# A GpSimd copy ahead of w_in's loads: issuing weights behind the turned k of batch 0

## Chip, cores and metric

One core of a Trainium2 chip. The metric is the device time of one execution in microseconds (us). The span of a profile is some 2 us shorter than the time of the same execution.

## The reference

Pooled attention, then a GELU layer. Inputs are float32.

```python
# q, k, v: (8 batches, 8 heads, 576, 64);  w_in: (512, 2048);  w_out: (2048, 512)
k_p, v_p = mean of k, v over groups of 8 rows              # 72 rows each
attn = softmax(q @ k_p.T / 8)
x = (attn @ v_p), heads side by side                       # (4608, 512)
out = gelu_tanh(x @ w_in) @ w_out
```

## The kernel before

Batch 0's attention runs alone at the start. Then 9 groups of 512 rows go through the two products, with the attention of the next batch in between. Weights are cast to bf16 by the DMAs that GpSimd issues; k and v of batch 0 come over the queues of SyncE and ScalarE.

```python
load_k(0, [nc.sync, nc.scalar])
load_v(0, [nc.sync, nc.scalar])
load_q(0, 0, 1)                       # GpSimd, as all loads down to w_out
load_q(0, 1, 2)
make_identity(nc, identb)
load_w_in(0)                          # first half of w_in: rows 0 to 255, used first
load_w_in(1)                          # second half
load_k(1, [nc.gpsimd])
load_q(1)
for i in range(4):                    # w_out in four parts
    nc.gpsimd.dma_start(out=w_out_b[...], in_=w_out_v[:, i])
# ...
trans_k_mm(0, 4, 0, KR, D)
trans_k_copy(0, 0, 4, upper=False)    # VectorE writes kTs[0][0]: the first part of the turned (transposed) k
trans_q(0, ...)
trans_k_copy(0, 1, 4, upper=False)
scores(0, 0, 2)
# ... scores, exponentials, denominators ...
for f in v_steps(0): f()              # VectorE adds up v
av0(0, 0, 4)                          # PE: attention times v (L368)
# ...
for i in range(2):
    nc.vector.memset(vts[1][:, 2 * i, 0:1], 0.0)
load_v(1, [nc.sync], 2)               # v of batch 1, issued once these memsets are done
for fo, ko in [(fo, ko) for fo in range(6) for ko in range(2)]:
    p1_mm(0, fo, ko)                  # 12 products with w_in's first half (L402)
# group 0 goes on with ko 2 and 3: w_in's second half; then p2_mm with w_out (L411)
```

The softmax here doesn't subtract the row's maximum and nothing guards it: scores larger than these inputs give would overflow.

Of the kernel before, what the change touches and what calls it, by code (L numbers as in the profile page):

```python
# [18 lines left out]
def kernel(  # L19
# [9 lines left out]
    nc = tc.nc  # L29
# [39 lines left out]
    def load_k(b, engs):  # L69
        rows = k[b].rearrange("h (j l) d -> (h j) (l d)", l=8)  # L70
        main = rows[0:128 * KR].rearrange("(p r) c -> p r c", r=KR)
        n = KR // len(engs)
        for i, eng in enumerate(engs):
            eng.dma_start(out=kts[b % 2][:, i * n:(i + 1) * n], in_=main[:, i * n:(i + 1) * n])
        engs[0].dma_start(out=kts[b % 2][64:128, KR], in_=rows[128 * KR:])
        rows = v[b].rearrange("h (j l) d -> j h (l d)", l=8)
        engs[-1].dma_start(out=kts[b % 2][0:64, KR], in_=rows[64:])  # L77
# [18 lines left out]
    def load_q(b, i0=0, i1=2):  # L96
        if b not in qs:
            qs[b] = qp.tile([128, 2, T * D], BF16, name="qb")
        nc.gpsimd.dma_start(
            out=qs[b][:, i0:i1],  # L100
            in_=q[b].rearrange("(i h) (p t) d -> (h p) i (t d)", i=2, t=T)[:, i0:i1])
# [3 lines left out]
    w_out_b = consts.tile([128, FO, DM], BF16, name="w_out_b")  # L105
    w_in_v = moe_w_in.rearrange("(ko p) f -> p ko f", p=128)
    w_out_v = moe_w_out.rearrange("(q p j) d -> p q (j d)", p=128, j=4)
# [9 lines left out]
    def load_w_in(i):  # L117
        nc.gpsimd.dma_start(out=w_in_b[i], in_=w_in_v[:, 2 * i:2 * i + 2])

    load_w_in(0)  # L120
    load_w_in(1)
    load_k(1, [nc.gpsimd])
    load_q(1)
    for i in range(4):
        nc.gpsimd.dma_start(out=w_out_b[:, 4 * i:4 * i + 4, :].rearrange("p j d -> p (j d)"), in_=w_out_v[:, i])
    gate = consts.tile([1, 2], BF16, name="gate")


    xT = consts.tile([128, KO, N], BF16, name="xT")

    kTs = [[consts.tile([128, H, Sp], BF16, name=f"kT{i}{e}") for e in range(2)] for i in range(2)]
# [78 lines left out]
    def half_bank(bank):  # L210
        return PS[:, bank, :].bitcast(BF16)
# [7 lines left out]
    def trans_k_copy(b, e, bank, lower=True, upper=True):  # L219
        tp = half_bank(bank)[0:D, 0:(KR + 1) * 128].rearrange("p (r c) -> p r c", c=128)  # L220
        o = kTs[b % 2][e][e * 64:(e + 1) * 64]

        def heads(h0, h1, n, c0, c1):
            nc.vector.tensor_copy(out=o[:, h0:h1, 0:n].rearrange("p h (j r) -> p h j r", r=KR),
                                  in_=tp[:, 0:KR, c0:c1].rearrange("p r (h j) -> p h j r", h=h1 - h0))

        if lower:
            heads(0, 4, Sp, 0, 4 * KH)
        if upper:
            heads(4, H - 1, Sp, 4 * KH, 7 * KH)  # L230
            heads(H - 1, H, 8, 7 * KH, 128)
            nc.vector.tensor_copy(out=o[:, H - 1, 8:Sp], in_=tp[:, KR, 64:128])
# [22 lines left out]
    def trans_q(b, i, t0, n, bank, eng):  # L255
        trans_q_mm(b, i, t0, n, bank)
        trans_q_copy(b, i, t0, n, bank, eng)
# [11 lines left out]
    def qk(b, c, pr, bank):  # L269
        for e in range(2):  # L270
            h = 2 * pr + e
            nc.tensor.matmul(out=PS[:Sp, bank + e, :CH].rearrange("j (t p) -> j t p", p=32),  # L272
                             lhsT=kTs[b % 2][c][:, h],
                             rhs=qTs[b][:, h // 4, :, h % 4 * 32:h % 4 * 32 + 32],
                             start=True, stop=True)

    def expo(b, c, pr, bank):
        e = ep.tile([Sp, 2, CH], BF16, name="e", bufs=8)
        nc.scalar.activation(out=e, in_=PS[:Sp, bank:bank + 2, :CH], func=ACT.Exp, scale=1.0 / 64.0)  # L279
        es[b, c, pr] = e  # L280
# [157 lines left out]
    def scores(c, pr, bank):  # L438
        qk(0, c, pr, bank)
        expo(0, c, pr, bank)  # L440
# [3 lines left out]
    trans_q(0, *QG[0], 5, nc.scalar)  # L444
    trans_q(0, *QG[1], 6, nc.vector)
    trans_k_copy(0, 1, 4, upper=False)
    scores(0, 0, 2)
    scores(0, 1, 0)
    spin(2, 7)
# [55 lines left out]
    for g in range(NG):  # L505
# [41 lines left out]
        if g + 1 == NG:  # L547
# [3 lines left out]
            for i, o in enumerate(gLs):  # L551
                side[4 * i + 3].append(lambda i=i, o=o: nc.vector.tensor_copy(  # L552
                    out=o.rearrange("p f (x t) -> p f t x", t=4),
                    in_=gTs[g][:, 4 * i:4 * i + 4, 384:].rearrange("p f (t x) -> p f t x", t=4)))
# [130 lines left out]
```

## Time and profile before

| | before |
|---|---|
| median of 3 runs | 301.98 us (301.66 to 302.01) |
| PE busy | 291.7 of 300.3 us |
| v of batch 0 landed | 16.3 us |
| first product with w_in | 21.25 us |
| w_in's halves landed | 17.1 and 23.1 us |

A DMA is finished when 16 engines have counted its semaphore up. The trace keeps the time of each count, so "landed" is the 16th, and where the 15th is given as well, the difference is how far one engine lags. "PE waits" are idle times of the engine just ahead of an instruction. The prediction shows the lines.

### The profile page before, as it was taken

How to read it: one execution, taken by the hardware profiler on the slowest of the kernel's cores; microseconds unless marked ns; L12 is line 12 of the kernel's file. 1: busy time of each engine (PE TensorE's matmuls, PEld its weight loads, DVE VectorE, ACT ScalarE, POOL GpSimd, SP SyncE). 2: the span in 40 equal slices, each digit the busy share in tenths (PEclk: the TensorE clock that was granted, in tenths of full speed). 3: DMA queues.
4: the chain of work that ended last, by engine and by line, in shares of the span. 5: the costliest groups of instructions: out<-in, count | busy, mean ns of one | idle time of the engine just before them, and what ended most of it. 6: DMA issues, size and time to landing. Idle time of an engine off the chain costs nothing.

```text
span 300.3 us, 4352 instructions
## 1 busy us (share of the span) xinstructions
PE 291.7 (97%) x1496; PEld 151.0 (50%) x1525; DVE 152.7 (51%) x308; ACT 217.1 (72%) x408; POOL 37.5 (12%) x67
## 2 busy tenths in 40 slices
PE   8889999999999999999999999999999999999995
PEld 3555545554555455545554555455545555445443
DVE  3766585574576257815690659155924630111112
ACT  1687678879888898789878988798879887206500
POOL 7104002300600060005000410033000000000000
PEclk9999999999999999999999999999999999999999
DMA  7999985981799269935984499729961210121022
GB/s 225 265 249 272 248 172 105 248 210 16 181 259 179 38 159 252 183 68 123 258 191 87 92 255 208 106 51 250 238 120 38 69 42 0 36 71 36 0 62 80
DMA packets 38790, 43.11 MB, mean 144 GB/s; under 512 B 25520, under 2 KB 26160, under 8 KB 38640
## 3 DMA queue, kind: packets, MB, share of 16 engines
q0 software_dynamic: 8000, 24.39, 35.7%
q1 hardware_dynamic: 30064, 17.06, 25.2%
q10 hardware_dynamic: 704, 1.38, 1.4%
q8 instruction: 12, 0.20, 0.3%
q14 instruction: 10, 0.08, 0.1%
HBM read 36.70 MB, written 9.44 MB: 154 GB/s over the span
## 4 chain that ended last, share of the span: by engine, by line
PE 91%; DMA 5%; DVE 2%; issue 1%; ACTq 1%
PE PS L402 41%; PE PS L411 39%; DMA vt<-in_v_dram 5%; PE PS L327 4%; PE PS L316 2%; PE PS L647 1%; DVE vt L154 1%; PE PS L301 1%; PE PS L368 1%; PE PS L292 1%; PE PS L272 0%; ACTq L77 0%; PE PS L241 0%; DVE xT L345 0%; PE PS L354 0%
## 5 line engine op out<-in xcount | busy, mean ns | idle before, releaser
L411 PE MATMUL PS<-w_out_b,gT 128*128 128x512 bf16 x543 | 134.7, 379 | 0.9 <-issue 0.2
L402 PE MATMUL PS<-xT,w_in_b 128*128 128x512 bf16 x565 | 125.7, 379 | 0.6
L408 ACT ACTIVATE gT<-PS 128x512 bf16<-128x512 f32 x144 | 79.6, 606 | 44.6 <-PE PS L402 44.6
L402 PEld LDWEIGHTS <-w_in_b 128*128 128x128 bf16 x576 | 65.0, 113 | 58.5
L411 PEld LDWEIGHTS <-gT 128*128 128x128 bf16 x560 | 53.9, 97 | 51.1 <-issue 1.7
L345 DVE TENSOR_TENSOR xT<-PS,rc 64x288 bf16<-64x288 f32 x112 | 51.0, 455 | 21.2 <-ACT rc L337 18.7
L417 DVE COPY osb<-PS 128x512 f32<-128x512 f32 x33 | 22.8, 692 | 48.1 <-PE PS L411 44.8
L322 ACT ACTIVATE eT<-PS 64x576 bf16<-64x576 f32 x48 | 30.7, 640 | 0.6
L309 DVE COPY eT<-er 8x576 bf16<-8x576 bf16 x24 | 7.3, 302 | 39.4 <-ACT er L307 38.9
L334 ACT ACTIVATE ld<-PS 64x288 f32<-64x288 f32 x56 | 22.5, 403 | 5.6 <-PE PS L327 5.1
L337 ACT ACTIVATE rc<-ld 128x288 f32<-128x288 f32 x56 | 24.8, 443 | 1.8
L379 ACT ACT_TABLE_LOAD x17 | 21.8, 1283 | 3.6 <-issue 3.3
L154 DVE TENSOR_TENSOR kt<-kt 128x1280 f32<-128x1280 f32 (+5 forms) x18 | 18.9, 1048 | 10.0 <-DMA kt<-in_v_dram 5.9
L335 ACT ACTIVATE ld<-PS 64x288 f32<-64x288 f32 x56 | 22.5, 403 | 1.4
L327 PE MATMUL PS<-eT,vp 72*128 72x288 bf16 x96 | 19.7, 285 | 0.1
L154 DVE TENSOR_TENSOR vt<-vt 128x512 f32<-128x512 f32 (+2 forms) x18 | 15.6, 865 | 2.1 <-DMA vt<-in_v_dram 1.8
L512 POOL COPY gate<-eT 1x2 bf16<-1x2 bf16 x5 | 0.9, 176 | 125.4 <-DMA eT<-er 125.4
L327 PEld LDWEIGHTS <-vp 72*128 72x128 bf16 x96 | 9.5, 98 | 11.3
L279 ACT ACTIVATE e<-PS 72x576 bf16<-72x576 f32 x16 | 9.9, 645 | 3.1 <-PE PS L272 2.9
L431 PE MATMUL PS<-idle 128*128 128x512 bf16 x30 | 9.9, 476 | 1.3 <-DVE idle L143 1.2
L316 PE MATMUL PS<-qT,kx 128*128 128x288 bf16 x48 | 9.8, 286 | 0.0
L552 DVE COPY kt<-gT 128x512 bf16<-128x512 bf16 x4 | 3.0, 747 | 11.5 <-ACT gT L408 11.5
(66 smaller groups left out, 131.0 us busy)
## 6 DMA issues: line engine op xcount, KB each, us to landing
out_dram<-osb SPq DMA_DIRECT2D x141, 64.0 KB
kt<-in_k_dram POOLq DMA_DIRECT2D x12, 512.0 KB, 6.2
vt<-in_v_dram POOLq DMA_DIRECT2D x12, 512.0 KB, 10.5
qb<-in_q_dram POOLq DMA_DIRECT2D x7, 576.0 KB, 14.4
w_in_b<-in_moe_w_in_dram POOLq DMA_DIRECT2D x2, 1024.0 KB, 16.7
w_out_b<-in_moe_w_out_dram POOLq DMA_DIRECT2D x4, 512.0 KB, 24.3
kt<-in_k_dram POOLq DMA_DIRECT2D x1, 1024.0 KB, 22.1
vt<-in_v_dram SPq DMA_DIRECT2D x4, 256.0 KB
```

The source lines that it names most:

```text
L154: nc.vector.tensor_tensor(out=o, in0=a, in1=b, op=ALU.add)
L322: nc.scalar.activation(out=eT[0:64, 2 * pr:2 * pr + 2, c, :], in_=PS[64 * c:64 * c + 64, 2:4, :CH], func=ACT.Exp, scale=1.0 / 64.0)
L327: nc.tensor.matmul(out=PS[:, bank + x, :CH], lhsT=window(vps[b % 2], 2 * pr + x), rhs=eT[:, 2 * pr + x, c, :], start=True, stop=True)
L334: nc.scalar.activation(out=ld[0:64], in_=PS[64:128, bank, :CH], func=ACT.Ln)
L335: nc.scalar.activation(out=ld[64:128], in_=PS[0:64, bank + 1, :CH], func=ACT.Ln)
L337: nc.scalar.activation(out=rc, in_=ld, func=ACT.Exp, scale=-1.0)
L345: nc.vector.tensor_tensor(out=xT[rows, pr, col:col + CH], in0=PS[rows, bank + x, :CH], in1=rc[rows], op=ALU.mult)
L379: nc.scalar.preload_act_table_set(name)
L402: nc.tensor.matmul(out=PS[:, h_bank(g, fo), :], lhsT=w, rhs=xT[:, ko, r0:r0 + GROUP], start=(ko == 0), stop=(ko == KO - 1))
L408: nc.scalar.activation(out=gTs[g][:, fo, :], in_=PS[:, h_bank(g, fo), :], func=ACT.Gelu_apprx_tanh)
L411: nc.tensor.matmul(out=PS[:, bank], lhsT=gTs[g][:, fo, r * 128:(r + 1) * 128], rhs=w_out_b[:, fo], start=(fo == first), stop=(fo == last))
L417: nc.vector.tensor_copy(out=osb, in_=PS[:, bank])
```

## The change

Its intent: w_in is not needed before 21 us, v is. So let w_in start only when q and v of batch 0 are nearly there.

```diff
-    load_w_in(0)
-    load_w_in(1)
-    load_k(1, [nc.gpsimd])
-    load_q(1)
-    for i in range(4):
-        nc.gpsimd.dma_start(out=w_out_b[...], in_=w_out_v[:, i])
     gate = consts.tile([1, 2], BF16, name="gate")
+
+    def load_rest():
+        load_w_in(0)
+        load_w_in(1)
+        load_k(1, [nc.gpsimd])
+        load_q(1)
+        for i in range(4):
+            nc.gpsimd.dma_start(out=w_out_b[...], in_=w_out_v[:, i])
 ...
     trans_k_copy(0, 1, 4, upper=False)
+
+    nc.gpsimd.tensor_copy(out=gate[0:1], in_=kTs[0][0][0:1, 0, 0:2])
+    load_rest()
     scores(0, 0, 2)
```

More of the change, by code (lines that the diff above doesn't have):

```diff
@@ L118, in load_w_in @@
         nc.gpsimd.dma_start(out=w_in_b[i], in_=w_in_v[:, 2 * i:2 * i + 2])
-    load_w_in(0)
-    load_w_in(1)
-    load_k(1, [nc.gpsimd])
-    load_q(1)
-    for i in range(4):
-        nc.gpsimd.dma_start(out=w_out_b[:, 4 * i:4 * i + 4, :].rearrange("p j d -> p (j d)"), in_=w_out_v[:, i])
-    gate = consts.tile([1, 2], BF16, name="gate")
+    gate = consts.tile([1, 2], BF16, name="gate")
+    def load_rest():
[4 more added lines that the diff above has]
+        for i in range(4):
+            nc.gpsimd.dma_start(out=w_out_b[:, 4 * i:4 * i + 4, :].rearrange("p j d -> p (j d)"), in_=w_out_v[:, i])
     xT = consts.tile([128, KO, N], BF16, name="xT")
```

## The prediction

> **What bounds the kernel now.** I read the page first (time by engine, then the chain that ended last), then that chain piece by piece for the first 24 us, then the timeline there, then the DMA queues in short stretches.
>
> The page says TensorE is the bound almost throughout, with one load in the chain:
>
> ```profile
> PE 291.7 (97%) x1496; PEld 151.0 (50%) x1525; DVE 152.7 (51%) x308; ACT 217.1 (72%) x408; POOL 37.5 (12%) x67
> ...
> PE 91%; DMA 5%; DVE 2%; issue 1%; ACTq 1%
> ```
>
> So a gain can only come from the start, where the chain is not PE. The chain in order of time (start us, length us, what):
>
> ```profile
> 2.62 13.69 DMA vt<-in_v_dram
> 16.31 0.02 issue
> 16.33 1.24 DVE vt L154
> 17.57 0.02 issue
> 17.59 0.70 DVE vt L154
> 18.29 0.03 issue
> 18.32 0.43 DVE vz L154
> 18.75 0.05 issue
> 18.79 1.16 PE PS L368 x8
> 19.95 0.49 PE PS L354 x4
> 20.44 0.98 PE PS L368 x8
> 21.42 1.94 PE PS L402 x9
> ```
>
> v of batch 0 lands at 16.31, VectorE adds it up, L368 multiplies by it, and L402 (the first product with w_in) then runs without a gap. What v is in a hurry for is a wait of VectorE of only 1.43 us; the same timeline shows what stands before it:
>
> ```profile
> 14.72 0.17 DVE L232 COPY kT<-PS 64x64 bf16<-64x64 bf16 x1
> ...
> 16.33 1.95 DVE L154 TENSOR_TENSOR vt<-vt 128x1024 f32<-128x1024 f32 x2 [1.43 <-DMA vt<-in_v_dram]
> ```
>
> w_in is issued at 3.03 and 3.74. Its two halves land after 14.1 and 19.3 us (least and most in the view of the tile), at 17.1 and 23.1. Only the issue is early, though. The DMA queues from 10.4 to 16.4 (packets, MB, share of the 16 engines):
>
> ```profile
> q0 software_dynamic: 276, 1.05, 86.7%
> q10 hardware_dynamic: 155, 0.28, 13.2%
> q1 hardware_dynamic: 98, 0.17, 8.4%
> ```
>
> q0 is GpSimd's ring (q, then w_in, in this order), q1 and q10 are SyncE's and ScalarE's (k, then v). The single packets of the trace show where q0 turns from q to w_in: q's are 2304 B, w_in's 4096 B. The first of w_in start at 10.0 to 10.7; q's second half lands at 11.4, its first at 8.6, k's main part at 6.0. So w_in never competed with k, and hardly with q, which stands ahead of it in the ring. It competes with the rest of v: 0.45 MB left at 10.4, 198 packets of 2 KB after 10.6. Those take some 90 ns each, a w_in packet 323 ns, and an engine takes them in turn; that is how 0.45 MB last until 16.3.
>
> **What the Trainium skill says.** "DMA: Bandwidth & Descriptors", section "Queues, rings and completion order": each DMA engine takes its rings round robin, a packet at a time, and consumes one ring in order. The trace agrees on both (the packet sizes above; from 12 to 13 us 39 packets of w_in beside 54 of v). The same page, "Specifications", gives about 1 us to the first byte of a DMA that GpSimd issues. The trace is slower: the k load that GpSimd issues at 76.19, on an idle q0, has its first packets at 77.4, moves 0.05 MB from 77.2 to 78.2 and 0.27 MB in the next us. So 1.2 us to the first packet, 2.0 us to full flow. "Perfetto Trace Analysis", section "DMA Instruction — SWDGE (GPSIMD)": the row of such a DMA is the writing of descriptors, not the movement. The trace agrees: 0.72 us of row, 14 us to landing. "SBUF — State Buffer", section "Who interferes with whom": VectorE copies in a two-port mode lock GpSimd out of descriptor writing. VectorE's copies at 10 to 15 us read PSUM, so I count nothing for it; GpSimd's row lengths (0.72 for a w_in half now) would show it.
>
> **The change part by part.** It removes no work. It adds one GpSimd copy of 1x2 (176 ns in the gate group of the page) and moves ten DMA issues behind it.
>
> 1. When they go out. The copy reads kT, whose first part VectorE writes from 9.05 to 9.50. Gate from about 9.55 to 9.73; a gate later in the kernel is followed by its first issue 0.35 to 0.43 us after its end (50.60+0.18 to 51.21); so w_in goes out at about 10.15 and 10.87, the rest by 14. First w_in packets 1.2 us later, 11.35; full flow 2.0 us later, 12.15. Now it is 10.6: a delay of 0.8 to 1.5 us.
>
> 2. v. Without w_in the rest of v needs (13.2% + 8.4%) x 6.0 us = 1.3 us of all engines, from 10.4 to 11.7 on average. v is unevenly spread (its last engine now is 1.1 us behind the one before it, 16.3 against 15.2) and the last packets will meet the first of w_in. v lands at 12.3 to 14.5.
>
> 3. What that is worth. k and q come as now, so VectorE is free for v at 14.9 as now, and v is there. The adds start 1.43 us earlier, and the first vz is ready at 14.9 + 2.42 = 17.3. Then PE takes over as the bound: before L368 it has two fillers (L431) that end at 17.25 + 0.60 = 17.85, held by the exponentials of ScalarE and not by v. L368 starts at 17.85 and not 18.79: 0.94 us gained, not 4 and not 1.43. Nothing behind it takes it back before w_in: ScalarE's reciprocal for the second part (19.14 to 19.82) and the banks that it frees are in time. L402 starts near 20.3 instead of 21.25.
>
> 4. What w_in's second half takes back. The first 12 L402 matmuls use the first half of w_in (12 x 0.216 = 2.6 us); the 13th wants the second, now at 23.85 against a landing at 23.1: 0.75 us of slack. Shifted by 0.94 it wants it at 22.9. Without a pause of the engines the landing stays at 23.1 (same bytes, same engines). But between 11.7, when v runs out, and 12.15, when w_in flows, they idle some 0.4 us on average, from 0 to 1.3. The second half lands at 23.1 to 24.4, mid value 23.5. The 13th matmul starts there instead of 23.85: -0.75 to +0.55 us, in the middle -0.35.
>
> 5. Behind that PE is its own bound; no later load gains. w_out's second part now lands at 37.5 and is wanted at about 38.3 (nine matmuls into L411), so it too has under 1 us of slack, and the same pause delays it.
>
> Sum: 301.98 - 0.94 (v) + 0.6 (w_in and what follows it in the ring) = 301.6.
>
> **Rivals.** (a) v was the whole problem, so its four or more us come through: 298 us. Against it: VectorE reaches v only at 14.9 and PE's own queue holds it to 17.85, neither of which reads v. (b) The wait moves from v to w_in: PE stops ahead of the 13th L402 matmul, and the time stays or rises by a us, 302 to 303. For it: 0.75 us of slack, a ring that starts anew behind a gate, and the first DMA of GpSimd in this kernel, issued at 1.25, whose first packets come only at 4.7 to 5.2, 3.5 us later. With 3.5 us here w_in would flow at 13.7, 2 us of pause, its second half at 25.1, and the kernel would lose 1.2 us: 303.2. (c) The first packets come fast, at 11.3, no pause at all: only the full 0.94 less 0.2 remains, 301.1. (d) q and k come sooner as well, since GpSimd writes no other descriptors; then the chain ahead of 14.9 shrinks and the time falls below 301. Against it: w_in's packets start behind q's already.
>
> **Range and chances.** 301.6 us; 8 times in 10 within 300.8 to 302.9, from (c) with a little of (d) to most of (b). 2% are 6 us. That much can't be gained: L402 starts at 21.25 and PE's chain up to 17.85 has no v in it. To lose it, w_in would have to come 6 us later than it does. Faster 0.02, same 0.96, slower 0.02.
>
> **What would show it.** Step 1: gate at 9.6 on GpSimd, w_in issues at 10.1 and 10.9, w_in's first packets at 11.3 to 12.2. Step 2: VectorE's wait for v gone, v landed by 14.5. Step 3: vt adds at 14.9, L368 at 17.9, L402 at 20.3. Step 4: a wait of PE for w_in ahead of the 13th L402 matmul, 0.2 to 1 us, and a DMA share under 1 near 12 us. Step 5: L411 at its old pace, perhaps a short wait for w_out. I am wrong if VectorE reaches v much before 14.9, if q or k land at other times than 8.6, 11.4 and 6.0, or if w_in's second half lands outside 23 to 24.4.

## The result

302.11 us (median of 6 runs, 301.59 to 303.34) against 301.82 (6 runs, 301.32 to 302.51). The ratio is 1.0015, 95% interval 0.9991 to 1.0039: no change. A ratio here is the mean time of one kernel's runs over that of the other's of the same rounds, so not quite the ratio of the medians. Executions over 1.5% slower than the fastest of the same kernel are left out of the means.

The timeline of the changed kernel (start us, length us, engine, line, operation; in brackets the idle time ahead of it and what ended it). Its L370, L404 and L413 are L368, L402 and L411 of the kernel before.

```profile
9.54 0.18 POOL L450 COPY gate<-kT 1x2 bf16<-1x2 bf16 x1 [6.46 <-DVE kT L226]
9.66 1.44 POOL L118 DMA_DIRECT2D w_in_b<-in_moe_w_in_dram  x2
...
14.90 1.95 DVE L156 TENSOR_TENSOR vt<-vt 128x1024 f32<-128x1024 f32 x2
...
17.66 1.14 PE L370 MATMUL PS<-e,vz 72*128 72x288 bf16 x8
...
20.11 2.75 PE L404 MATMUL PS<-xT,w_in_b 128*128 128x512 bf16 x11
...
23.54 8.82 PE L404 MATMUL PS<-xT,w_in_b 128*128 128x512 bf16 x40 [0.68 <-DMA w_in_b<-in_moe_w_in_dram]
...
38.89 1.46 PE L413 MATMUL PS<-w_out_b,gT 128*128 128x512 bf16 x6 [0.68 <-DMA w_out_b<-in_moe_w_out_dram]
```

Against the corresponding line of the kernel before:

```profile
21.25 11.39 PE L402 MATMUL PS<-xT,w_in_b 128*128 128x512 bf16 x51
```

VectorE's wait for v is gone (14.90, no bracket). PE starts with w_in 1.14 us sooner. Then it stops twice, where it had not stopped before: after 12 products (11 are in this trace, a few records are missing) for w_in's second half, and after eight products with w_out for w_out's second part. In the kernel before, the first stretch with w_in is one row of 11.39 us; here it is two. The page's chain, the work that ended last followed back from the end, now runs through w_out's load instead of v's: PE's share fell from 91%, DMA's rose from 5%. A DMA counts there from its issue, so the 8% (w_out's second part from 14.1 to 38.9) is not the length of the waits.

```profile
PE 87%; DMA 8%; POOL 2%; DVE 1%; issue 1%
```

Counted out between the two profiled executions: PE is 1.14 us ahead at the first product with w_in, 0.31 ahead at the 13th (23.54 against the 23.85 that the prediction worked out), 0.28 ahead at the first product with w_out (35.85 against 36.13), and 0.42 behind at its last instruction (296.93 against 296.51). So 0.83 us are given back at w_in, 0.70 at w_out. The two executions took 302.74 and 302.29.

The gap that the gate makes in GpSimd's ring can be seen in the DMA queues from 10.5 to 11.0 us. First the kernel before, then the changed one (packets, MB, share of the 16 engines):

```profile
q0 software_dynamic: 28, 0.06, 57.6%
q10 hardware_dynamic: 28, 0.06, 29.4%
q1 hardware_dynamic: 26, 0.05, 29.4%
```

```profile
q1 hardware_dynamic: 47, 0.10, 54.5%
q10 hardware_dynamic: 44, 0.09, 50.3%
q0 software_dynamic: 9, 0.00, 1.0%
```

With q0 empty, v moves at 1.7 times the rate (91 packets instead of 54). But then the single packets show a slow start: w_in's first packet starts at 11.19, and its packets take 897 ns on average from 11.0 to 11.5, 595 to 12.0, 401 to 12.5, 392 to 13.0, and about 330 only from there on.

### The profile page after: what moved, and what is told of

The parts are those of the page before. It is cut to its first block, busy times and chain, and to the rows that moved or that the text cites. A ratio compares the mean times of both kernels' runs of the same rounds, so it can differ in the third digit from the quotient of the medians.

```text
span 300.7 us, 4353 instructions
## 1 busy us (share of the span) xinstructions
PE 291.8 (97%) x1496; PEld 151.1 (50%) x1525; DVE 152.7 (51%) x308; ACT 217.1 (72%) x408; POOL 37.8 (13%) x68
## 4 chain that ended last, share of the span: by engine, by line
PE 87%; DMA 8%; POOL 2%; DVE 1%; issue 1%
PE PS L413 39%; PE PS L404 37%; DMA w_out_b<-in_moe_w_out_dram 8%; PE PS L329 4%; PE PS L433 2%; PE PS L318 2%; PE PS L652 1%; PE PS L303 1%; PE PS L294 1%; POOL w_in_b L118 0%; PE PS L274 0%; DVE vt L156 0%; DVE xT L347 0%; POOL qb L99 0%; POOL kt L77 0%
## 5 line engine op out<-in xcount | busy, mean ns | idle before, releaser
L413 PE MATMUL PS<-w_out_b,gT 128*128 128x512 bf16 x543 | 134.9, 379 | 1.6 <-DMA w_out_b<-in_moe_w_out_dram 0.7
L404 PE MATMUL PS<-xT,w_in_b 128*128 128x512 bf16 x565 | 125.9, 379 | 1.3 <-DMA w_in_b<-in_moe_w_in_dram 0.7
L404 PEld LDWEIGHTS <-w_in_b 128*128 128x128 bf16 x576 | 64.9, 113 | 59.5 <-DMA w_in_b<-in_moe_w_in_dram 1.2
L413 PEld LDWEIGHTS <-gT 128*128 128x128 bf16 x560 | 53.9, 97 | 52.0 <-issue 2.7
L336 ACT ACTIVATE ld<-PS 64x288 f32<-64x288 f32 x56 | 22.6, 403 | 5.5 <-PE PS L329 5.0
L337 ACT ACTIVATE ld<-PS 64x288 f32<-64x288 f32 x56 | 22.6, 403 | 1.4
L329 PEld LDWEIGHTS <-vp 72*128 72x128 bf16 x96 | 9.5, 98 | 11.3
## 6 DMA issues: line engine op xcount, KB each, us to landing
vt<-in_v_dram POOLq DMA_DIRECT2D x12, 512.0 KB, 10.5
qb<-in_q_dram POOLq DMA_DIRECT2D x7, 576.0 KB, 14.9
w_in_b<-in_moe_w_in_dram POOLq DMA_DIRECT2D x2, 1024.0 KB, 10.5
w_out_b<-in_moe_w_out_dram POOLq DMA_DIRECT2D x4, 512.0 KB, 22.6
```

The costliest lines, as they stand in the source:

```text
L329: nc.tensor.matmul(out=PS[:, bank + x, :CH], lhsT=window(vps[b % 2], 2 * pr + x), rhs=eT[:, 2 * pr + x, c, :], start=True, stop=True)
L336: nc.scalar.activation(out=ld[0:64], in_=PS[64:128, bank, :CH], func=ACT.Ln)
L337: nc.scalar.activation(out=ld[64:128], in_=PS[0:64, bank + 1, :CH], func=ACT.Ln)
L404: nc.tensor.matmul(out=PS[:, h_bank(g, fo), :], lhsT=w, rhs=xT[:, ko, r0:r0 + GROUP], start=(ko == 0), stop=(ko == KO - 1))
L413: nc.tensor.matmul(out=PS[:, bank], lhsT=gTs[g][:, fo, r * 128:(r + 1) * 128], rhs=w_out_b[:, fo], start=(fo == first), stop=(fo == last))
```

## The experiments

Two theories. **Given back:** v's gain is real, but w_in and w_out come over a ring that is busy from 5 to 43 us, nearly just in time, so every pause ahead of them comes back as a wait of PE. **Nothing gained:** the start of w_in's product does not set the end. What the pause is (the gate, or something beside it) and how much of v's lateness is chance are the finer questions. The diffs are against the changed kernel unless said otherwise.

This table holds the profiled executions for all that follows: last count of v of batch 0, first product with w_in, last count (and 15th) of w_in's second half and PE's wait for it, the same for w_out's second part, all in us. A profile shows one execution, and three of the gated ones were slow for their kernel: those of the changed kernel (302.74, the second slowest of six), of gate_on_pooled_k and of w_in_six_to_eight (the slowest of six). Their waits are at the upper end.

| kernel | v | first w_in product | w_in 2nd half (15th) | PE waits | w_out 2nd part (15th) | PE waits |
|---|---|---|---|---|---|---|
| before, first profile | 16.3 | 21.25 | 23.1 (22.0) | 0 | 37.5 (35.1) | 0 |
| before_again | 15.3 | 20.34 | 22.6 (22.3) | 0 | 36.8 (36.1) | 0 |
| ungated_eight | 15.1 | 20.04 | 22.6 (22.1) | 0 | 36.6 (36.5) | 0 |
| ungated_no_w2 | 15.5 | 20.49 | not loaded | 0 | 29.5 (29.3) | 0 |
| changed | 12.9 | 20.11 | 23.5 (22.4) | 0.68 | 38.9 (36.3) | 0.68 |
| gated_no_w2_again | 13.0 | 19.84 | not loaded | 0 | 30.4 (29.7) | 0 |
| gate_on_pooled_k | 13.3 | 20.03 | 23.4 (22.5) | 0.70 | 39.0 (36.6) | 0.76 |
| gate_one_us_later | 12.9 | 19.98 | 24.6 (24.0) | 1.96 | 40.4 (38.3) | 0 |
| gated_v1_later | 12.9 | 19.94 | 23.0 (22.3) | 0.39 | 35.8 (35.2) | 0 |
| w_in_six_to_eight | 13.7 | 20.02 | 23.3 (22.7) | 0 | 38.4 (37.1) | 0.65 |
| eight_and_v1_as_before | 12.9 | 19.83 | 23.0 (22.2) | 0 | 37.5 (35.6) | 0.43 |
| v_in_the_q_ring_eight (no gate) | 14.9 | 19.94 | 24.2 (23.9) | 0.68 | 39.5 (39.1) | 0.97 |

### Without w_in's second half: is v's gain worth anything?

The same cut was made in the kernel before, as the control. Their outputs are wrong, which doesn't matter for the times.

```diff
-        load_w_in(1)
 ...
-        w = w_in_b[ko // 2][:, ko % 2, ...]
+        w = w_in_b[0][:, ko % 2, ...]
```

> The changed kernel without the load of w_in's second half (the first half is used twice; the result is wrong on purpose). Given-back theory: v's gain is real and is lost again to the loads behind the gate; with those 5 us sooner nothing takes it back, so PE reaches the first w_in product at 20.1, does not stop at the 13th or for w_out, and the time is 300.6 to 301.1, 0.8 to 1.2 us under its own control (the kernel before with the same cut). Rival, nothing was gained: the start of w_in's product does not set the end, and this run and its control come out within 0.3 us of each other.

> Control for the run above: the kernel before without the load of w_in's second half (wrong result on purpose). Given-back theory: w_in's first half still runs beside v, which lands at 16 to 16.5, PE reaches the first w_in product at 21.3, and since PE had no wait for w_in or w_out the time stays at 301.6 to 302.0. Rival: if this one gets faster too, some load behind w_in was a hidden bound of the kernel before.

The gated kernel: 300.99 us over all 6 runs, of which the profiled one took 628.01 us and is no use (see the last section); the five fast ones have the median 300.85. The control: 301.08 (6 runs, 300.83 to 301.32), not the 301.6 to 302.0 expected. The difference, 0.2 us, is within the 0.3 that the rival named, so by the times alone the rival stands. The control's own rival came true in small: its ratio to the kernel before is 0.9981 (0.9969 to 0.9993), so something behind w_in did hold the kernel before up; more on this below. Since the first profile was lost, the gated kernel ran again:

> The changed kernel without w_in's second half once more (wrong result on purpose), for a profile of a fast execution: its first one fell on an execution of twice the length. Given-back theory: v lands near 13, PE reaches the first w_in product at 20.1 and shows no wait over 0.3 us up to 45 us; the control reached it at 20.65 with v at 15.5, so the time is 300.5 to 300.9, 0.2 to 0.6 us under the control's 301.08. Rival: PE starts at 20.1 and still ends like the control; then a wait before 50 us must show where it went.

300.96 us (4 runs, 300.78 to 301.01). The control's timeline, then the gated kernel's:

```profile
15.57 1.95 DVE L153 TENSOR_TENSOR vt<-vt 128x1024 f32<-128x1024 f32 x2 [0.76 <-DMA vt<-in_v_dram]
...
18.03 1.15 PE L367 MATMUL PS<-e,vz 72*128 72x288 bf16 x8 [0.27 <-DVE vz L153]
...
20.49 11.39 PE L401 MATMUL PS<-xT,w_in_b 128*128 128x512 bf16 x52
```

```profile
14.63 1.95 DVE L155 TENSOR_TENSOR vt<-vt 128x1024 f32<-128x1024 f32 x2
...
19.84 11.39 PE L403 MATMUL PS<-xT,w_in_b 128*128 128x512 bf16 x52
```

Two things follow. The lead at the first product with w_in (19.84 against 20.49: 0.65 us) is still there at PE's last instruction (294.94 against 295.60: 0.66), and PE shows no new wait. So a lead at that point does reach the end when nothing behind it is late; "nothing gained" falls, in this pair of profiles. But the lead is small: in the control v landed at 15.5, not 16.3, and PE waited 0.27 us for it, not 0.95. The medians, 0.1 to 0.2 us apart, say that it is often smaller still.

Part of what held the kernel before up is seen in the weight loads of PE, whose records are complete. From the first one with w_in to the last one with the GELU output it is 271.36 us in both kernels without the second half, but 271.51 and 271.69 in the two profiles of the kernel before. The 0.15 and 0.33 us stand ahead of L292, the first product with batch 1's pooled v: it starts 0.40 and 0.58 us after the L272 ahead of it, 0.25 in the control. L292 also needs a small move (8 KB of pooled rows, issued on ScalarE's queue at 31.88 and 30.97), and that landed at 39.89 and 39.15, 0.13 and 0.14 us before L292 started. So even the kernel before waited a little for a DMA, though not for w_in or w_out.

### The kernel before once more: is v at 16.3 its property?

No edit.

> The kernel before against itself, for a second profile and for the noise. If v's landing at 16.3 is a property of the kernel: 16.0 to 16.6 again, PE's wait ahead of L368 0.7 to 1.0 us. If the last engine's place is chance: a landing from 15.0 to 16.6, and a smaller wait; the gain to be had from v is then smaller in most executions than the first profile shows. Ratio 0.9985 to 1.0015.

301.86 us (4 runs), ratio 1.0005 (0.9991 to 1.0020). The second profile:

```profile
15.32 1.95 DVE L154 TENSOR_TENSOR vt<-vt 128x1024 f32<-128x1024 f32 x2 [0.21 <-DMA vt<-in_v_dram]
...
20.34 11.39 PE L402 MATMUL PS<-xT,w_in_b 128*128 128x512 bf16 x52
```

It was chance. Of four profiles without a gate, v landed at 16.3, 15.5, 15.3 and 15.1; with the gate at 12.9 to 13.7. The first product with w_in is at 20.04 to 20.49 in three of the ungated profiles, at 19.83 to 20.11 in the seven gated ones of the table. How much of this is v's can be read off: L368 comes after two pairs of fillers (L431, matmuls on an idle tile, which wait for no v). In all seven gated profiles it starts 0.43 or 0.44 us after the last pair starts; in the four without a gate 1.55 (the first profile), 0.87 (ungated_no_w2), 0.47 (ungated_eight) and 0.44 (before_again). So v cost PE 1.1 us in the profile that the prediction had, 0.4 in the control without the half, and next to nothing in the other two: VectorE waited there for v, but PE did not. What else separates the first products with w_in lies in the start of the fillers (16.95 to 17.46), that is ahead of v.

### The gate 1.04 us later: is w_in on the path?

```diff
-    nc.gpsimd.tensor_copy(out=gate[0:1], in_=kTs[0][0][0:1, 0, 0:2])
+    nc.gpsimd.tensor_copy(out=gate[0:1], in_=kTs[0][1][64:65, 0, 0:2])
```

> The gate reads the other half of the turned k, written 1.04 us later (10.09 to 10.54), so w_in goes out at 10.7. Given-back theory with the pause as the cost: w_in's second half lands 0.8 to 1.1 us later than in the changed kernel, at 24.3 to 24.6, PE's wait for it grows from 0.7 to 1.5 to 1.8 us, time 302.8 to 303.2. Rival, the engines have other work to fill the pause with: landing within 0.3 us of 23.5, time 302.0 to 302.3.

304.54 us (4 runs, 303.95 to 304.86), ratio 1.0093 (1.0076 to 1.0111): slower than expected.

```profile
11.03 1.44 POOL L118 DMA_DIRECT2D w_in_b<-in_moe_w_in_dram  x2
...
24.70 8.82 PE L404 MATMUL PS<-xT,w_in_b 128*128 128x512 bf16 x40 [1.96 <-DMA w_in_b<-in_moe_w_in_dram]
```

The issue is 1.37 us later than in the changed kernel (11.03 against 9.66), w_in's second half 1.2 us (24.65 against 23.49), and PE's wait grew by 1.28, while v landed where it did. So a pause ahead of w_in costs about its own length: the given-back theory holds for w_in. On top, PE waits 0.46 us for batch 1's pooled k and 0.30 for w_out's first part, which shows that the whole ring is late. The profiled executions differ by 1.5 us (304.26 and 302.74), the medians by 2.4; three of the four runs had a granted clock of 0.987 to 0.993, so part of the 2.4 may not be the gate's.

### The gate 1 us earlier: does the pause go away?

```diff
     for f in k_steps(0, slice(0, KR)):
         f()
+    nc.gpsimd.tensor_copy(out=gate[0:1], in_=kps[0][0:1, 0, 0:2])
+    load_rest()
 ...
-    nc.gpsimd.tensor_copy(out=gate[0:1], in_=kTs[0][0][0:1, 0, 0:2])
-    load_rest()
```

> The gate reads the pooled k (kp, written at 8.4) instead of the turned k (9.5), so w_in is issued at 8.6 and queues behind q. Pause theory: the ring never runs dry, w_in's packets start at 10.6 as in the kernel before, v lands at 15 to 16.3, w_in's second half at 23.1, w_out's second part at 37.5, PE reaches the first w_in product at 20.8 to 21.3, time 301.6 to 302.0: the gate then does nothing. Rival, the gate helps through the descriptors that GpSimd no longer writes early: v lands near 13 here too, with no pause, and the time falls to 301.0 to 301.4.

301.93 us (6 runs, 301.74 to 302.87), ratio 1.0011 (0.9997 to 1.0026). The time is the one that the pause theory named, but not for its reason: the landings are those of the changed kernel (v at 13.3, w_in at 23.4, w_out at 39.0), not those of the kernel before. GpSimd's issue, and the queues from 10.5 to 11.0 us:

```profile
8.63 1.44 POOL L118 DMA_DIRECT2D w_in_b<-in_moe_w_in_dram  x2
```

```profile
q10 hardware_dynamic: 45, 0.09, 51.9%
q1 hardware_dynamic: 45, 0.09, 51.5%
q0 software_dynamic: 8, 0.00, 0.9%
```

w_in was issued 1.8 us before q's last packet started (10.4) and still q0 ran dry: w_in's first packet came at 11.1, 2.5 us after the issue. In the changed kernel it came at 11.2, 1.5 us after it; with the gate 1 us later, when q was done, at 12.4, 1.4 us after it. An issue 1.03 us sooner gained 0.1 us. Part of the 2.5 us is the wait behind q. Why the ring then still pauses, no run here tells. The slow start was small in this run: 348 ns from 11.0 to 11.5, 428 at most after that.

### v in w_in's own ring: can the pause be had for nothing?

Against the kernel before, without a gate: v stands between q and w_in in one ring, so w_in follows it without a new start. A second run has in addition eight groups on w_in's first half (the edit of the next experiment).

```diff
-    load_v(0, [nc.sync, nc.scalar])
     load_q(0, 0, 1)
     load_q(0, 1, 2)
+    load_v(0, [nc.gpsimd])
     make_identity(nc, identb)
```

> No gate; the kernel before with batch 0's v issued by GpSimd between q and w_in, so that w_in stands behind v in one ring and follows it without a pause. Given-back theory with the pause as the cost: v lands at 11.5 to 13, VectorE starts on it at 14.9, PE reaches the first w_in product at 20.1 to 20.3, w_in's second half lands at 22.0 to 23.1 (no pause), w_out's second part at 37.0 to 37.8; PE waits 0 to 0.4 us for each; time 301.0 to 301.4. Rival, starting PE 1 us earlier cannot help because the ring's bytes set the landing of w_out whatever comes first: 301.6 to 302.0.

> The run above with eight groups begun on w_in's first half. Given-back theory: no wait for w_in, at most 0.3 us for w_out; time 300.8 to 301.2, under both kernels. Rival, the bytes set w_out's landing: as the run above, 301.6 to 302.0.

304.19 us (4 fast runs; the profiled one, 345.49, fell in a slow execution) and 304.34 (6 runs, 303.50 to 304.93), ratios 1.0081 and 1.0086. Both expectations missed, and v landed at 14.9, not at 11.5 to 13. The second run's queue from 10 to 15 us, and PE's waits:

```profile
q0 software_dynamic: 293, 1.07, 106.4%
```

```profile
24.24 7.96 PE L402 MATMUL PS<-xT,w_in_b 128*128 128x512 bf16 x36 [0.68 <-DMA w_in_b<-in_moe_w_in_dram]
...
39.53 1.46 PE L411 MATMUL PS<-w_out_b,gT 128*128 128x512 bf16 x6 [0.97 <-DMA w_out_b<-in_moe_w_out_dram]
```

v in GpSimd's ring moves in packets of 4 KB of some 300 ns; on the other two rings the same bytes are two packets of 2 KB of about 90 ns each. v's 1.05 MB are 256 such packets: by estimate 256 x 300 / 16 = 4.8 us of all engines instead of 512 x 90 / 16 = 2.9. Such a surplus of some 1.9 us fits what is seen downstream: w_in's second half at 24.2 instead of 22.6 in before_again, w_out's second part at 39.5 instead of 36.8. No pause, but more work for the engines, and PE waits in the same two places. It is the landing of those two that counts, here too.

### More work on w_in's first half: does removing one wait help?

```diff
-    for fo, ko in [(fo, ko) for fo in range(6) for ko in range(2)]:
+    for fo, ko in [(fo, ko) for fo in range(8) for ko in range(2)]:
 ...
-            first = [(fo, ko) for fo in range(6) for ko in (2, 3)]
+            first = [(fo, ko) for fo in range(8) for ko in (2, 3)]
 ...
-            if fo >= (5 if g else 6):
+            if fo >= (5 if g else 8):
```

> The changed kernel with eight instead of six groups of w_in's product begun on w_in's first half (16 instead of 12 matmuls before the second half is wanted). Given-back theory: PE wants the second half at 23.57, where it lands, so the first wait (0.68 us) goes; the second one, for w_out's second part at 38.9, grows by about as much to 1.2 to 1.4 us; time 301.8 to 302.2, no change against the changed kernel. Rival, each wait costs by itself: time 301.3 to 301.5.

301.40 us (6 runs, 301.04 to 302.63), ratio to the kernel before 0.9991 (0.9977 to 1.0006). The median is 0.7 us under the changed kernel's, where the rival put it; the two were not timed in the same rounds, and the profiled execution (302.63) was the slowest of the six. In that one the wait for w_in is gone, and others stand in its place:

```profile
31.80 0.45 PE L219 MATMUL PS<-identb,kp 128*128 128x128 bf16 x5 [0.40 <-DVE kp L156]
...
38.47 1.46 PE L413 MATMUL PS<-w_out_b,gT 128*128 128x512 bf16 x6 [0.65 <-DMA w_out_b<-in_moe_w_out_dram]
```

So part moved to batch 1's k, as given back says, and the wait for w_out did not grow. How much the edit gains in a usual execution stays open. The control, the same edit in the kernel before:

> Control: the kernel before with eight groups begun on w_in's first half. Given-back theory: it had no wait for w_in, so nothing changes: ratio 0.9985 to 1.0015, 301.4 to 301.9. Rival, the eight groups help by themselves (fewer switches): 301.1 or less.

301.45 us (4 runs, 301.14 to 301.95), ratio 0.9992 (0.9979 to 1.0006): as expected for a kernel that had no wait for w_in. Gated and ungated, the version with eight groups takes the same time, 301.40 and 301.45. With the first wait taken out, the gate is still worth nothing.

### Batch 1's v: who delays w_out?

v of batch 1 goes out on SyncE when its memsets are done, and these follow the last work of batch 0 on VectorE. In the changed kernel that work was done 1 us sooner than in the first profile of the kernel before, so these loads go out at 22.72 instead of 23.68 and take turns with k, q and w_out. Moved back:

```diff
-    for i in range(2):
-        nc.vector.memset(vts[1][:, 2 * i, 0:1], 0.0)
-    load_v(1, [nc.sync], 2)
     for w in vps:
         nc.vector.memset(w, 8.0)
+    for i in range(2):
+        nc.vector.memset(vts[1][:, 2 * i, 0:1], 0.0)
+    load_v(1, [nc.sync], 2)
```

> The changed kernel with the loads of batch 1's v issued some 2 us later (their small memsets behind those of vp). Theory that the wait for w_out comes from v of batch 1 now going out 1 us sooner: w_out's second part lands at 37.5 to 38 instead of 38.9, PE's wait of 0.7 us for it goes, time 301.3 to 301.6. Rival, it comes from the pause of the ring alone: w_out still lands near 38.9, time 302.0 to 302.2. The wait for w_in (0.7 us, second half at 23.5) stays in both.

303.35 us (6 runs, 302.92 to 303.59), ratio 1.0054 (1.0042 to 1.0067). The landing was sooner than expected, 35.8, and the wait for w_out is gone. The time was missed:

```profile
42.31 1.15 DVE L156 TENSOR_TENSOR vt<-vt 128x512 f32<-128x512 f32 x2 [1.25 <-DMA vt<-in_v_dram]
...
44.64 0.28 PE L294 MATMUL PS<-e,vp 72*128 72x288 bf16 x1 [1.19 <-DVE xT L347]
```

Now v of batch 1 itself is late, at 42.2, and PE waits 1.19 us for what hangs on it. The move was 2 us; the next run makes it smaller, by putting the memsets between the two of vp, with eight groups as well:

> The changed kernel with eight groups begun on w_in's first half, and batch 1's v issued at the time that it has in the kernel before (its memsets after the first of vp's, near 23.7 instead of 22.7). Theory that the earlier v of batch 1 is what delays w_out: w_out's second part lands at 37.5 to 38.0 and PE waits at most 0.3 us for it, time 300.8 to 301.1, 0.3 us or more under the run with eight groups alone (301.4). Rival, the delay is the ring's own: w_out at 38.4 or later, time 301.3 to 301.6.

301.85 us (4 runs, 301.69 to 302.04), ratio 1.0004 (0.9989 to 1.0018). It missed its 300.8 to 301.1. v of batch 1 went out at 23.51 and w_out's second part landed at 37.5, as expected, but PE, with its first wait gone, was there sooner:

```profile
37.49 1.46 PE L413 MATMUL PS<-w_out_b,gT 128*128 128x512 bf16 x6 [0.43 <-DMA w_out_b<-in_moe_w_out_dram]
```

PE waits once more at 43.21, 0.22 us, for batch 1's attention, and is then at the same place as before_again to the hundredth (43.70). No order of these transfers that was tried beats the kernel before by more than the noise: in the kernel before, w_in's second half (landed 23.1, wanted 23.85), w_out's second part (37.5, 38.3) and the last of batch 1's v (40.8, 41.6) are each wanted within 0.8 us of when they land.

The 15th count shows what this order is worth. With v of batch 1 out at 23.5 or later it is at 35.1 to 35.6, with or without the gate; with v out at 22.6 to 23.0 it is at 36.1 to 37.1 (in kernels that load all of w_in, without gate_one_us_later and v_in_the_q_ring_eight, whose whole ring is late), again with or without. But before_again and ungated_eight have that v out at 22.96 and 22.61 without any gate, and their w_out lands at 36.8 and 36.6. So the early v explains the later landing only against the first profile; against the other two, what is left of w_out's lateness is mostly its last engine.

What this leaves open: in the gated profiles with v of batch 1 at its early place, w_out's last engine lags the 15th by 1.3 to 2.5 us where all of w_in is loaded; in two of the three ungated ones that load all of w_in by 0.7 and 0.1, in the third by 2.4. The lag begins at w_in's second half. The trace of every fast execution has one 16 KB packet of 0.9 to 1.4 us on the instruction queue, starting at 20.0 to 20.4 us, also the two with the smallest lag, so it is no explanation by itself; the trace does not say which engine carries it. Whether the gate makes the lag worse or seven profiles fell that way is not settled.

## Why the prediction was right

The time, 302.11, lies within 300.8 to 302.9, and "same" was given 0.96. Point by point:

1. **When w_in goes out.** The gate was at 9.54 as said. The issue followed at 9.66 and not 10.15, and still the first packet came at 11.19, against the 11.35 said: an issue 0.5 us too late in the sum and a way to the first packet 0.3 us too short (1.5, not 1.2) made up for each other, which is luck. (In the k load that it was modelled on, the first packet starts at 77.52 and not 77.4, 1.3 us after the issue.) The full flow, said at 12.15, came at about 13: the restart was slower than its model. GpSimd's rows stayed at 0.72 us each, so no lock-out by VectorE shows.
2. **v.** 12.9, within 12.3 to 14.5.
3. **What that is worth.** VectorE at 14.90 (said 14.9), L370 at 17.66 (17.85), L404 at 20.11 (20.3): the mechanism and its limits, VectorE free only at 14.9 and the fillers ahead of L370, were right. The size, 0.94 us, was near the 1.14 against the one profile at hand and too large as a forecast: that profile caught v's slowest engine about a us later than the other three ungated ones. This is the first mis-sized term; in those three v cost PE 0.4, 0.03 and 0 us.
4. **What w_in takes back.** Landing 23.5 (said 23.5, range 23.1 to 24.4), a wait of 0.68 us (said 0.2 to 1), the 13th product at 23.54. Right, and confirmed by the gate 1 us later. The two other ungated profiles that load it have it at 22.6, the gated ones, the later gate aside, at 23.0 to 23.5, so the landing costs 0.4 to 0.9 us in a usual pair, where the sum set 0.4.
5. **What w_out takes back.** "Perhaps a short wait" was right in kind. The term was mis-sized: the sum had 0.6 us for w_in and all that follows it, 0.83 and 0.70 were measured in the pair of profiles. Two parts were not seen: that VectorE's earlier end releases batch 1's v sooner than in the first profile, which takes turns with w_out (with this load later, w_out landed at 37.5 and 35.8 instead of 38.4 to 39.0), and the lag of w_out's last engine, whose cause stays open.

So the sum of -0.34 came out at +0.4 in the profiled pair and +0.3 in the medians. With an interval of 0.9991 to 1.0039 the sign stays open. The gain was sized on an unlucky draw and the cost too small; the range was wide enough to hold the time all the same. Of the rivals, (a), 298 us, fell as said: no wait of PE's before 17.66 reads v. (b), the wait that moves to w_in, is the one that came, with a wait of 0.68 us, and the time lies in its 302 to 303. (c), no pause at all, fell: the first packets were as early as it said and then slow. (d) fell: q's halves landed at 8.7 and 11.3, k's main part at 5.9.

## What to carry to other kernels

Where the DMA engines are busy from the first load to the last early consumer, as here, holding one load back for another may only choose which consumer waits; look for the slack of every load behind the gate, in order of landing, before counting the gain of the one ahead of it. A restart of a ring was not free here, and an engine that gets done sooner may release a load that competes with the one you just delayed. One profile is one draw: the landing of the last of 16 DMA engines moved by 1.2 us between executions of kernels that load v alike, as much as the whole gain that was hoped for, so profile the kernel before twice before sizing such a change, and ask whether the engine that sets the time waits for the load, not only the engine that reads it.

## What the Trainium skill lacked or had wrong

- "DMA: Bandwidth & Descriptors", section "Specifications", has about 1 us to the first byte of a GpSimd DMA. Here it was 1.3 us (76.19 to 77.52) and 1.4 us (11.03 to 12.4) on a ring that had run dry. In the first half us after that, packets took 1.0 us on average with the gate 1 us later, 0.9 in the changed kernel and 0.35 in gate_on_pooled_k, instead of 0.32; that page does not mention the slow start.
- The same page, section "Issuing engines are not separate DMA queues", says that issuing from several engines saves only the sequencer's issue time. Here the choice of ring changed the engines' own time: 1.05 MB of v cost, by estimate, some 4.8 us of all engines in GpSimd's ring (4 KB packets of 300 ns) and 2.9 us on SyncE's and ScalarE's (2 KB of 90 ns), and the kernel was 2.5 us slower. Ring and packet size changed together; no run parts them.
- The same page, section "Latency and other measured facts", knows of slower single engines, but not how far they move: w_out's second part had its last engine 0.1 to 2.5 us behind the 15th.
- "TensorE: Matmul & The Clock Gate", section "Part 1: The HAM clock gate (the "warmup" mystery)", explains a half-rate PE by idle windows (and warns, further down, that the traced clock events can be unreliable). One execution of 628.01 us had PE busy 99% of its span and 52 products with w_in in 24.59 us, 0.47 us each against 0.22, while the profile listed a granted clock of 1.0. No run here explains it.
